# mLSTM cell and leaky-ReLU feed-forward: x of three steps of the second chunk transposed by VectorE and fetched through DRAM

## The chip, the core and the metric

The kernel runs on one core of a Trainium2 chip. The metric is the device time of one execution in microseconds. A core has five engines with instruction streams of their own: TensorE (PE: matrix products and transposes, with weight loads as PEld), VectorE (DVE), ScalarE (ACT), GpSimd (POOL) and SyncE (SP), which here does nothing but issue transfers between DRAM and the on-chip memory. ScalarE issues some transfers too. All transfers are carried out by sixteen DMA engines.

## The reference

An mLSTM cell runs over 4 batches, 8 heads, 768 positions and a head width of 40, and its output goes through two matrix products with a leaky ReLU between them:

```
m_new  = max(f + m, i)                      # gates, per head and position
C      = exp(f + m - m_new) * C + exp(i - m_new) * outer(v, k)
n      = exp(f + m - m_new) * n + exp(i - m_new) * k
y      = sigmoid(o) * (C q) / max(|n.q|, 1)
x      = y as (4 * 768 tokens, 320)
h      = x @ w_in                           # 320 -> 2048
out    = max(0.01 h, h) @ w_out             # 2048 -> 320
```

## The kernel before

The 768 positions are worked in six chunks of 128. A chunk has four steps, one per batch, so steps 0 to 3 are the first chunk, 4 to 7 the second, and so on to 23. A step yields x, 128 tokens by 320 columns. The feed-forward of a chunk takes its four steps together: `xT`, x transposed, with 512 tokens in the free dimension (step b of the chunk in columns 128 b to 128 b + 127), is multiplied by pieces of `w_in` (products `ph`), goes through the leaky ReLU into `acts`, and is multiplied by `w_out` (products `po`).

`xT` has five slots of 128 partitions by 512 tokens. Slot k holds rows 64 k to 64 k + 127 of the transposed x; the tile of x is 384 columns wide, with its first 64 columns repeated at the end, so that the last slot wraps round.

Cell and feed-forward are interleaved by hand: while the feed-forward of chunk c - 1 runs, the cell of chunk c is slipped in between. The loop at the end (L1471 to L1559) goes over the feed-forward's units i, runs unit i, then runs those units of the cell whose place is at most i. The list `cell_units` (L1270) says which units the cell of a chunk has, and `place` (L1461) where those of the second chunk stand. TensorE, VectorE, ScalarE and GpSimd execute in the order in which this code emits their instructions. SyncE's order is made by a scheduler, and stands fixed in the built program; there each of its transfers also waits for the one eight places before it.

For the second chunk (steps 4 to 7) the units of a step are `u_parts` (L707: scores and states on TensorE, their products on VectorE), `u_plain` (L776: the output `hN` on TensorE, its division by the denominator on VectorE and GpSimd, which gives the tile x, named `x` for steps 4 and 5 and `hn` for 6 and 7), and `u_x` (L851). `u_x` turns the 128x384 tile with five TensorE transposes (L860) into PSUM, from where ScalarE copies it into the step's columns of `xT` (L861, L862). All four `u_x` of the chunk come at the end, at places 22, 24, 26 and 28, when the feed-forward of the first chunk does its `po` products (L894).

Chunks three to six do it otherwise: their `u_mix` (L802) gives x already turned, writes it to the DRAM tile `x_dr`, and `gather_x` (L837) reads it from there into `xT`, both on SyncE's queue.

The next stage is `fast_firsts` (L1017) for the second chunk. Its first products (`p2`, then `p1`; matmuls at L1033) read the first 256 columns of `xT`, which are steps 4 and 5. Before it, `sums_of_x` (L1010) has GpSimd make sums of all four steps' columns (L1015); the third kind of product (`p6`) is the first to read those. `w_in` and `w_out` arrive as 64-bit numbers in the tile `raw` and are narrowed by ScalarE and VectorE (L302 to L311) in small pieces between the units. The loads for the third chunk (tiles `rb`, `ea`, `kn`, `S`, `w`) are issued on SyncE's queue while the second chunk's steps finish.

Of the kernel before, what the change touches and what calls it, by code (L numbers as in the profile page):

```python
# [8 lines left out]
F32 = mybir.dt.float32  # L9
# [9 lines left out]
def kernel(  # L19
# [26 lines left out]
    nc = tc.nc  # L46
    B, H, S, D = q.shape
    P = 128
# [5 lines left out]
    DP = 64  # L54
    D1 = D + 1
    QW = 32
    DB = D // 2
    XW = Dm + DP
    V1 = DB + 1
    TB = P // QW  # L60
# [5 lines left out]
    GT = B * P  # L66
    KF = Dm // P
    KR = Dm - KF * P
    KC = Dm // DP
# [10 lines left out]
    wk = ctx.enter_context(tc.tile_pool(name="wk", bufs=2))  # L80
    psf = ctx.enter_context(tc.tile_pool(name="psf", bufs=4, space=PSUM))
    psc = ctx.enter_context(tc.tile_pool(name="psc", bufs=4, space=PSUM))
    dr = ctx.enter_context(tc.tile_pool(name="dr", bufs=1, space=bass.MemoryType.DRAM))
# [17 lines left out]
    sync, by_act = queues = Ordered(nc.sync), Ordered(nc.scalar)  # L101
# [113 lines left out]
    raw_l = raw_t[:].bitcast(F32)  # L215
# [97 lines left out]

    a_dr = dr.tile([NB, 2, 2, BH, SL], F32, name="a_dr")
    x_dr = dr.tile([NS, Dm, P], F32, name="x_dr")
    gT, gL, dCs = {}, {}, {}
    m0s = {}
    bus = {}
# [68 lines left out]
    st = {}  # L387
# [449 lines left out]
    def gather_x(s):  # L837
# [6 lines left out]
        for r in range(2):  # L844
            at = 0
            while at < KC:
                k0, n = run_of(r, at)
                sync.dma_start(xT[DP * r : DP * (r + 1), at : at + n, ts(b, P)], src[:, k0 : k0 + n, :])
                at += n

    def u_x(s, last=None):  # L851

        c, b = divmod(s, B)
        if b == 0:
            st["xT", c] = wk.tile([P, KC, GT], F32, name="xT", bufs=1)
        x, xT, tok = st[s]["x"], st["xT", c], ts(b, P)
        low = psc.tile([P, 2, P], F32, name="xt", tag="c")
        high = psc.tile([P, KC - 2, P], F32, name="xe", tag="c")
        for t, n, at in ((low, 0, 0), (low, 1, DP), (high, 0, 2 * DP), (high, 1, 3 * DP), (high, 2, 4 * DP)):
            nc.tensor.transpose(t[:, n, :], x[:, at : at + P], ident[:])  # L860
        nc.scalar.copy(xT[:, :2, tok], low[:])  # L861
        (last or nc.scalar.copy)(xT[:, 2:, tok], high[:])  # L862
        if c > 0:
            del st[s]
# [404 lines left out]

    def cell_units(c):  # L1270
        if c == 1:
            units = [(fn, c * B + n) for n in range(B) for fn in (u_parts, u_plain)]
            units.insert(2 * B - 2, (u_gates, c + 1))
            return units + [(u_x, s) for s in range(B, 2 * B)]
        units = [(fn, c * B + n + m) for n in range(0, B, 2) for fn in (u_parts, u_mix) for m in range(2)]
        if c + 1 < NB:
            units.insert(2 * B - 2, (u_gates, c + 1))
        return units
# [57 lines left out]
    def first_chunk():  # L1336
# [49 lines left out]
        state(1)  # L1386
        run(w, 2)
        u_x(0)
        gate(1)
        run(w, 4)  # L1390
        u_x(1)
        state_copy(0)
        state_copy(1)
# [39 lines left out]
    with tc.manual_schedule(engines={E.PE, E.DVE, E.Activation, E.Pool}):  # L1433
# [24 lines left out]

        ffs = ffs[2:]
        fetch = {6: [3, 4], 10: [5, 6], 16: [7]}  # L1460
        place = (6, 7, 9, 11, 14, 16, 17, 19, 21, 22, 24, 26, 28)  # L1461
        late = {}
        masks = {0: (2, 3), 14: (4, 5)}
        first_pairs = (1, 1, 3, 3, 13, 13, 17, 17, 17)
# [6 lines left out]
        for c in range(1, NB + 1):  # L1471
            if c > 1:
                ffs = ff_units(c - 1)
            cells = cell_units(c) if c < NB else []
            n_ff, n_c = len(ffs), len(cells)
            done = fed = 0
# [19 lines left out]
            for i in range(n_ff):  # L1496
# [50 lines left out]
                while fed < done:  # L1547
                    fn, s = cells[fed]
# [42 lines left out]
```

## Time and profile before

| | us |
|---|---|
| median of 3 runs | 472.44 |
| lowest and highest | 471.0, 474.79 |
| the profiled execution | 471.96 |
| its span | 470.2 |

| engine | busy us | share of the span |
|---|---|---|
| TensorE, products | 459.6 | 98% |
| TensorE, weight loads | 412.5 | 88% |
| VectorE | 365.4 | 78% |
| ScalarE | 206.6 | 44% |
| GpSimd | 170.1 | 36% |

The profile is of one execution. Its times start at 0 with the span; the execution's own time has 1.8 us more than the span. Views that are quoted: the page's busy times and its forty slices (a digit is the busy share in tenths); the chain of waits in order of time (start, length, engine, tile and line, count); timelines (start, length, engine, line, operation, tiles written and read, count, and in brackets the idle time before and what ended it); and the DMA queues in a stretch of time (queue, packets, megabytes, share of sixteen engines). The granted TensorE clock is full throughout.

### The profile page before, as it was taken

The numbers are of one execution on the slowest core, as the hardware profiler recorded it, in microseconds if no ns is written. First come the engines' busy times: TensorE is split into PE (matmuls) and PEld (weight loads), VectorE is DVE, ScalarE is ACT, GpSimd is POOL, SyncE is SP. The second block draws the span as 40 slices with busy tenths as digits, with TensorE's granted clock in tenths as the row PEclk, the third lists the DMA queues.
The fourth block names the chain that finished last, engine by engine and source line by source line (L and its number), as shares of the span: only waits on it lengthen the run. The fifth ranks groups of instructions, "written<-read, shape, count | busy, mean of one in ns | idle before, by whom it ended". The sixth has DMA issues, their size and how long they took to land.

```text
span 470.2 us, 14195 instructions
## 1 busy us (share of the span) xinstructions
PE 459.6 (98%) x5700; PEld 412.5 (88%) x5700; DVE 365.4 (78%) x676; ACT 206.6 (44%) x507; POOL 170.1 (36%) x219
## 2 busy tenths in 40 slices
PE   8988989999999999999999999999999999999997
PEld 5777878767788999988899988899988899988997
DVE  6778578998579999768689778689757687495886
ACT  4657878755337511356411367411356411153410
POOL 6230487264335154933214933214833004400000
PEclk9999999999999999999999999999999999999999
DMA  9999977878742594865654956654776213100001
GB/s 128 169 179 179 214 181 230 207 158 164 147 141 55 151 181 107 186 141 134 166 133 84 197 127 140 179 110 100 176 142 125 75 30 85 57 1 1 1 1 56
DMA packets 160849, 59.21 MB, mean 126 GB/s; under 512 B 123792, under 2 KB 152208, under 8 KB 160784
## 3 DMA queue, kind: packets, MB, share of 16 engines
q1 hardware_dynamic: 120800, 51.15, 49.3%
q10 hardware_dynamic: 39984, 7.17, 9.3%
q8 instruction: 45, 0.74, 0.7%
q14 instruction: 20, 0.16, 0.1%
HBM read 51.58 MB, written 6.70 MB: 124 GB/s over the span
## 4 chain that ended last, share of the span: by engine, by line
PE 88%; DMA 5%; SPq 3%; POOL 1%; issue 1%; ACT 0%; DVE 0%; POOLq 0%; DVEq 0%
PE ph L1033 33%; PE po L931 26%; PE po L894 8%; PE pl L1236 6%; PE pT L813 3%; SPq L95 3%; PE ph L872 3%; PE sd L725 3%; DMA kn<-in_k_dram 3%; DMA acts<-in_moe_w_in_dram 1%; DMA w<-a_dr 1%; PE sd L731 1%; PE tk L638 1%; PE hN L785 1%; PE tkq L652 0%
## 5 line engine op out<-in xcount | busy, mean ns | idle before, releaser
L1033 PE MATMUL ph<-xT,w_in 64*128 64x256 f32 x720 | 82.7, 378 | 0.0
L1033 PEld LDWEIGHTS ph<-xT,w_in 64*128 64x128 f32 x720 | 69.2, 187 | 8.6 <-issue 0.6
L931 PE MATMUL po<-w_out,acts 128*128 128x160 f32 x512 | 71.3, 300 | 0.0
L931 PEld LDWEIGHTS po<-w_out,acts 128*128 128x128 f32 x512 | 69.9, 190 | 0.3
L1062 DVE TENSOR_TENSOR acts<-acts,ph 128x512 f32<-128x512 f32 x60 | 38.4, 683 | 22.8 <-PE ph L1033 22.7
L1066 ACT COPY acts<-ph 128x512 f32<-128x512 f32 x60 | 32.2, 588 | 49.7 <-PE ph L1033 49.7
L931 PE MATMUL po<-raw,acts 128*128 128x160 f32 x384 | 53.2, 300 | 0.0
L537 POOL TENSOR_SCALAR_AFFINE_SELECT w<-w 64x512 f32<-64x512 f32 x40 | 34.4, 861 | 51.3 <-DMA w<-a_dr 40.5
L931 PEld LDWEIGHTS po<-raw,acts 128*128 128x128 f32 x384 | 52.3, 190 | 0.3
L1058 ACT ACTIVATE acts<-acts 128x1024 f32<-128x1024 f32 x30 | 31.6, 1055 | 40.3 <-DVE acts L1062 30.8
L701 POOL TENSOR_TENSOR S<-S,f 40x336 f32<-40x336 f32 x36 | 30.6, 849 | 48.4 <-PE pT L813 32.7
L547 ACT ACTIVATE w<-w,gT 128x64 f32<-128x64 f32 x160 | 41.6, 337 | 13.1 <-DMA a_dr<-a 4.2
L742 DVE TENSOR_TENSOR qn<-w,sd 64x384 f32<-64x384 f32 (+1 forms) x80 | 33.4, 418 | 14.7 <-ACT acts L1066 7.8
L872 PE MATMUL ph<-xT,w_in 64*128 64x256 f32 x320 | 37.8, 383 | 0.0
L894 PE MATMUL po<-w_out,acts 128*128 128x320 f32 x128 | 36.7, 437 | 0.0
L1033 PE MATMUL ph<-acts,w 64*128 64x256 f32 x320 | 36.3, 379 | 0.0
L827 POOL TENSOR_TENSOR xb<-xb,den 128x320 f32<-128x320 f32 x16 | 11.6, 728 | 67.0 <-DVE xb L824 64.7
L872 PEld LDWEIGHTS ph<-xT,w_in 64*128 64x128 f32 x320 | 31.5, 187 | 3.8 <-ACT acts L880 0.4
L1033 PEld LDWEIGHTS ph<-acts,w 64*128 64x128 f32 x320 | 30.6, 187 | 3.6
L894 PEld LDWEIGHTS po<-w_out,acts 128*128 128x128 f32 x128 | 23.5, 190 | 9.2 <-ACT acts L880 0.3
L612 DVE TENSOR_TENSOR qn<-kqT,ea 64x512 f32<-64x512 f32 x32 | 30.0, 938 | 0.8
L1033 PE MATMUL ph<-xT,raw 64*128 64x256 f32 x240 | 26.8, 376 | 0.0
(267 smaller groups left out, 807.2 us busy)
## 6 DMA issues: line engine op xcount, KB each, us to landing
rb<-in_k_dram SPq DMA_DIRECT2D x64, 80.0 KB
rb<-in_q_dram SPq DMA_DIRECT2D x64, 80.0 KB
rb<-in_o_gate_dram SPq DMA_DIRECT2D x64, 80.0 KB
ea<-a_dr SPq DMA_DIRECT2D x32, 128.0 KB
raw<-in_moe_w_out_dram SPq DMA_DIRECT2D x6, 640.0 KB
w<-a_dr ACTq DMA_DIRECT2D x24, 128.0 KB
x_dr<-x SPq DMA_DIRECT2D x64, 40.0 KB
xT<-x_dr SPq DMA_DIRECT2D x16, 160.0 KB
```

Of the source, the lines that this page charges most:

```text
L537: nc.gpsimd.affine_select(part, part, compare_op=ALU.is_ge, fill=-1e30, base=0, pattern=[[0, H], [1, SL]], channel_multiplier=-1,)
L547: yield nc.scalar.activation(w[:, h, :], w[:, h, :], AF.Exp, bias=gT[c][:, 0, bh : bh + 1], scale=1.0)
L612: nc.vector.tensor_tensor(mixed(s)[rows, 1 - r], d["kqT"][rows, 1].rearrange("p (h t) -> p h t", t=SL), d["ea"][rows], op=ALU.mult,)
L701: nc.gpsimd.tensor_tensor(new, old, g, op=ALU.mult)
L742: nc.vector.tensor_tensor(mixed(s)[toks, u, hs], w[toks, hs], bank[1 - u][to[u][hs.start], hs], op=ALU.mult,)
L872: nc.tensor.matmul(ph[r][:, cols], lhsT=w_row(r, slot, j), rhs=xT[DP * r : DP * (r + 1), slot, cols], start=(slot == 0), stop=(slot == KC ...
L894: nc.tensor.matmul(po[n][:], lhsT=acts[:, f, ts(n, P)], rhs=w_out[:, f, :], start=(f == 0), stop=(f == NF - 1),)
L931: nc.tensor.matmul(bank[:], lhsT=left[:, f, :], rhs=right[:, f, :], start=f == 0, stop=f == KH - 1)
L1033: nc.tensor.matmul(bank[r][:, e, :], lhsT=left(r)[rows, e], rhs=right(r)[rows], start=first and e == 0 and m == 0, stop=e == 1 and m == le ...
L1058: nc.scalar.activation(to, z, AF.Prelu, alpha=0.01)
L1062: nc.vector.tensor_tensor(to[:, 2 * r : 2 * r + 2], to[:, 2 * r : 2 * r + 2], bank[r], op=ALU.add)
L1066: nc.scalar.copy(to[:, 2 * r : 2 * r + 2], bank[r])
```

## The change

For steps 4, 5 and 6 `u_x` is replaced by three units. `u_turn` has VectorE transpose the 128x384 tile of x in 32x32 blocks, each in its place, into a part of `raw` that the weights have left. `u_send` writes the blocks to a new DRAM tile `x1_dr`, one transfer for each of the four groups of 32 partitions; the blocks come to stand in DRAM in the order of the whole transpose, in pieces of 32 numbers (128 B). Steps 4 and 5 are sent together, step 6 alone. `u_gather` reads each step back into its columns of `xT` with one transfer over 128 partitions, five rows of 512 B in each, rows that belong to two slots being read twice. Step 7 keeps `u_x`. The places in the list are new: the transposes at 15 (twice) and 18, the sends at 16 and 19, the gathers at 19 and 20, the other units of the cell where they were, and the last `u_x` at 27 in place of 28.

```
+    x1_dr = dr.tile([B - 1, XW, P], F32, name="x1_dr")
...
+    def in_lines(s, n=1):
+        return raw_l[:, (s - B) * XW : (s - B + n) * XW]
+
+    def u_turn(s):
+        nc.vector.transpose(in_lines(s), st[s]["x"])
+        del st[s]
+
+    def u_send(s, n):
+        to = x1_dr[s - B : s - B + n].rearrange("b (j d) (i t) -> i d (b j) t", d=QW, t=QW)
+        for i in range(TB):
+            sync.dma_start(to[i], in_lines(s, n)[ts(i, QW)].rearrange("p (n t) -> p n t", t=QW))
+
+    def u_gather(s, n):
+        if s == B:
+            st["xT", 1] = wk.tile([P, KC, GT], F32, name="xT", bufs=1)
+        for n in range(s - B, s - B + n):
+            rows = bass.AP(x1_dr.tensor, x1_dr[n].offset, [[P, P], [DP * P, KC], [1, P]])
+            sync.dma_start(st["xT", 1][:, :, ts(n, P)], rows)
...
     def u_x(s, last=None):
         c, b = divmod(s, B)
-        if b == 0:
+        if s == 0:
...
         if c == 1:
-            units = [(fn, c * B + n) for n in range(B) for fn in (u_parts, u_plain)]
-            units.insert(2 * B - 2, (u_gates, c + 1))
-            return units + [(u_x, s) for s in range(B, 2 * B)]
+            (p0, x0), (p1, x1), (p2, x2), (p3, x3) = (((u_parts, s), (u_plain, s)) for s in range(B, 2 * B))
+            t0, t1, t2 = ((u_turn, s) for s in range(B, 2 * B - 1))
+            w01, w2 = ((lambda s, n=n: u_send(s, n), s) for s, n in ((B, 2), (B + 2, 1)))
+            g01, g2 = ((lambda s, n=n: u_gather(s, n), s) for s, n in ((B, 2), (B + 2, 1)))
+            t3 = u_x, 2 * B - 1
+            return [p0, x0, p1, x1, p2, t0, t1, w01, x2, (u_gates, c + 1), t2, p3, w2, g01, g2, x3, t3]
...
-        place = (6, 7, 9, 11, 14, 16, 17, 19, 21, 22, 24, 26, 28)
+        place = (6, 7, 9, 11, 14, 15, 15, 16, 16, 17, 18, 19, 19, 19, 20, 21, 27)
```

## The prediction

> **What bounds the kernel now.** I read the page first (busy times and slices), then the chain of waits over 80 to 180 us, then the timelines of TensorE, SyncE and VectorE around the four steps that the change touches, and last the trace's own records of DMA packets and of semaphore updates, which tell when each transfer landed.
>
> ```profile
> PE 459.6 (98%) x5700; PEld 412.5 (88%) x5700; DVE 365.4 (78%) x676; ACT 206.6 (44%) x507; POOL 170.1 (36%) x219
> PE   8988989999999999999999999999999999999997
> ```
>
> TensorE is full from the seventh slice on; in its own instructions the last gap over 0.04 us ends at 69 us. So from there the end is set by how much TensorE must do, and a piece taken out of it is worth its whole length, as long as nothing it later needs becomes late. The chain shows the pieces:
>
> ```profile
> 108.67 0.22 PE xt L860 x2
> 108.89 0.33 PE xe L860 x3
> 109.22 4.31 PE po L894 x16
> 113.52 0.22 PE xt L860 x2
> 113.74 0.33 PE xe L860 x3
> ...
> 123.78 2.15 PE po L894 x8
> 125.94 1.06 PE ph L1033 x8
> ```
>
> Each `u_x` is five transposes in 0.22 + 0.33 = 0.55 us. The last line is the first product of the next stage, the first reader of the second chunk's `xT`; its instruction starts at 125.87.
>
> **What it removes.** Three of the four `u_x`: 3 x 0.55 = 1.65 us of TensorE, all on the path. Their six ScalarE copies (373 and 482 ns each, 2.6 us) go as well; ScalarE waits there for the transposes, so they are worth nothing. The fourth `u_x` stays, one place earlier; its x is ready at about 114 us and TensorE doesn't wait for it. Without anything else the first product would start at 125.87 - 1.65 = 124.22.
>
> **What it adds to VectorE.** Three 32x32-block transposes of 128x384. No row has that shape; 128x512 took 690 ns at L604, 717 at L820 and 1140 at L831, whose output is scattered most. The new ones read and write plain rows, so I take L604's 384/512 x 690 = 0.52 us each, with 0.86 (from L831) as the upper end; nothing excludes a little less than 0.52, since all three rows have scattered sides. In the changed program's order two stand behind the L311 that ended at 90.76, the third behind the one at 98.82. VectorE has no idle time there until 107.69, so all that follows shifts by up to 3 x 0.52 = 1.56:
>
> ```profile
> 101.64 1.72 DVE L742 TENSOR_TENSOR qn<-w,sd 64x448 f32<-64x448 f32 x4
> 103.39 0.50 DVE L705 TENSOR_TENSOR S<-S,sd 40x336 f32<-40x336 f32 x1
> ```
>
> The L705 ends at 103.89, and TensorE's `hN` of step 7, which needs it, starts at 105.19. With 1.56 it ends at 105.45: TensorE waits about 0.3 us (with 0.86 per transpose, 1.3). At 107.69 VectorE had waited 0.98 for a weight load, so only 0.6 us is carried on, and its idle stretch after 124.65 (7.78 us) swallows that.
>
> **What it adds to SyncE's queue.** Eight writes and three gathers. In the program's order the four writes of steps 4 and 5 stand behind the first of the two `ea` loads of the first line below, the four of step 6 behind the `w` loads of the second, then the gathers, and the `rb` loads of the third only after them:
>
> ```profile
> 104.84 1.12 SPq L95 DMA_DIRECT2D ea<-a_dr  x2
> ...
> 114.29 1.28 SPq L95 DMA_DIRECT2D w<-a_dr  x2
> 115.66 2.01 SPq L95 DMA_DIRECT2D rb<-in_k_dram  x4
> ```
>
> SyncE issues without a pause there, one transfer per 0.35 to 0.65 us, so a place in the queue is a time. The blocks are ready long before (VectorE at about 91.8 and 100.4), so the queue decides. First `ea` issued at 105.4; four writes at the pace of four 32-partition loads (2.0) to 107.4; then what before took from 105.36 to 115.56 (10.2) to 117.6; four writes to 119.6; two gathers at the median 0.61 of `xT<-x_dr`, so the second starts at 120.2. Such gathers landed 3.1 to 5.1 us after the start of their issue (semaphore records, 169 to 178 us, a crowded stretch), the loads at 114 to 121 us 2.2 to 3.2. Between 3.2 and 5.1 the middle gives 124.4.
>
> The new packets lengthen this. The writes are 12 x 32 x 4 = 1536 packets of 128 B per step, 4608 in all. For their price, 111.5 to 116.5 us (mostly 80 B and 160 B loads) and 144 to 150 us (512 B writes to `x_dr`), queue, packets, MB and share of sixteen DMA engines:
>
> ```profile
> q1 hardware_dynamic: 3446, 0.57, 69.8%
> ...
> q1 hardware_dynamic: 548, 0.25, 17.3%
> ```
>
> The first is 0.698 x 16 x 5 us / 3446 = 16.2 ns for 165 B on average, the second 0.173 x 16 x 6 / 548 = 30.3 ns. The packet records agree: median 12 ns at 80 B, 14 at 160 B, 18 for the 256 B writes of `a_dr`. I take 14 ns, by size the nearest row: 4608 x 14 / 16 = 4.0 us of all engines. The idle share between 105.4 and 120 is 13% and 29% in the table by stretches, 0.6 + 2.9 = 3.5 us. So the writes fit but for 0.5 us, and the gather of step 5 **lands at about 125.0** (124.4 + 0.5). Each further ns per packet adds 4608 / 16 = 0.29 us.
>
> The Trainium skill, "DMA: Bandwidth & Descriptors", Specifications, says that transfers under 512 B make the engine read, modify and write; it speaks against these 128 B writes. If that doubled a packet to 28 ns, the sum would end at a landing of 129.0. The 256 B writes at 18 ns don't bear it out.
>
> **The sum.** TensorE reaches the first product at 125.87 - 1.65 + 0.3 = 124.5 and waits for the listed semaphores of the gathers of steps 4 and 5 until about 125.1. The start moves from 125.87 to 125.1: **a gain of about 0.75 us** of the 1.65. The two waits share: a longer one at `hN` shortens the other. The gather of step 6 waits for its writes to land (issued to 119.6, landing at 122.4 or so) and lands near 126; it and the remaining `u_x` feed GpSimd's sums, which in the run before started at 125.31 and are first read by TensorE at 138.88. Ten us of cover.
>
> Behind the gathers the queue is about 7 us late (2.0 + 2.0 + 3 x 0.61, and the wait of about 1.5 for landings). The tightest is step 11's `w`, landed at 130.61 before, 138 after; GpSimd's masks (L537, at 130.56) stand in front of its L701 at 137.64, which VectorE reads at 142.44. Masks until 139, L701 until 140: covered. The loads for VectorE's transposes at 148 to 153 landed by 134.4, so they have over 10 us.
>
> The profiled execution took 471.96 (span 470.2 and 1.8 around it), which the sum makes 471.2. The median of the runs is 472.44, 0.5 above that execution; against it, **471.7 us**.
>
> **The rivals.**
> - *The gather comes too late, slower than before.* One mechanism: the first product waits for the gather of step 5, and what passes 125.8 is a loss. It decides at a packet price of 14 + 0.8 / 0.29 = 17 ns. At the 30.3 ns of the `x_dr` writes the landing is 125.0 + 16.3 x 0.29 = 129.7, a loss of 3.9 us: 476.3. For it: those are this kernel's writes of x to DRAM, and SyncE has at most eight transfers under way, as each waits in the program's list for the one eight before it, so a slow write also holds up the issue. Against it: the packets grow dearer with size, and the 256 B writes cost 18. By the Trainium skill's rule (28 ns) the loss would be 3.2 us, 475.6. Chance 0.35.
> - *All of the 1.65 us but the 0.3 is kept.* The gathers land after 3.2 us as the lightly crowded loads did, by 124.5: 471.1. It belongs to the forecast's side, of which it is the better end.
> - *A covered wait loses its cover:* the transposes at 0.86 us and SyncE's 7 us grown to over 10, so that the masks hold L701, then VectorE's state and, at 161 us, TensorE's scores. No TensorE reader comes earlier, so it costs 0 to 3 us, 472 to 475. Chance 0.07.
> - *The transposes stay or the work moves elsewhere:* the program's order shows 15 fewer transposes before the first product, so no chance is kept for it.
>
> **How the numbers follow.** The forecast with its better end, net -1.65 to 0, has 0.55; the late gather 0.35; lost cover 0.07; 0.03 is left for what I don't see. The range runs from 470.2 (the full 1.65 off the median, and 0.6 for a median of few runs that spread from 471.0 to 474.79) to 476.0, nearly the late gather at 30.3 ns. A measurement of this kernel can tell about 1%, 4.7 us. A gain over 1% isn't in the work removed: 0.03. A loss over 1% needs a landing after 130.6, a packet price of 33 ns (the median of single `x_dr` packets is 34), or several losses together: 0.11. Within 1%: 0.86.
>
> **What would show it.** 15 fewer L860 transposes in the chain and 16 `po` matmuls following one another without them; the three new block transposes near 0.52 us; `hN` of step 7 waiting 0.3 us for VectorE; the first product waiting under 1 us for a DMA into `xT`; SyncE's `rb` loads starting near 122.5 in place of 115.66. It is wrong if that product waits over 1.5 us, or if TensorE has gaps after 126 us.

## The result and the profile after

| | before | after |
|---|---|---|
| median, us | 472.69 (6 runs) | 493.40 (6 runs) |
| lowest and highest | 471.0, 474.79 | 490.29, 499.72 |
| the profiled execution | 471.96 | 499.72 |
| its span | 470.2 | 497.9 |

The changed kernel is slower by a factor of 1.0425, with a 95% interval of 1.0375 to 1.0476: 20.7 us of the median, where the forecast was a gain of 0.75 and the range ended at 476.0. The profiled execution is the longest of the six, so its own loss is larger, 27.7 us of span; e1_both below shows the same later waits in an execution near its median. Ratios and intervals, here and below, leave out single executions far above the others of their kernel: 499.72 here, one of the kernel before at 530.78 and one of e8_softpin at 2672 us.

The page of the kernel after: busy times, two of the rows of forty slices (TensorE's busy tenths and the clock that it was granted), and the shares of the chain that ended last. Line numbers move with every edit (L1015 of the kernel before is L1039 here), and the profile leaves numbers out of tile names, so that `x1_dr` stands in it as `x_dr`.

```profile
PE 467.0 (94%) x5685; PEld 417.8 (84%) x5685; DVE 364.7 (73%) x679; ACT 203.9 (41%) x501; POOL 162.7 (33%) x219
PE   8998999999699999899999599999849999999997
...
PEclk9999999999799999999999979999959999999999
...
PE 59%; DMA 17%; SPq 14%; DVE 4%; POOL 3%; issue 2%; ACT 1%; ACTq 0%; DVEq 0%; POOLq 0%
```

TensorE's row had been full from the seventh slice on. Now it has dips in the slices 11, 17, 23 and 29 to 30, one at each start of a stage but the last, and the clock's row has dips in 11, 24 and 30. Although 15 products have gone, TensorE is busy for 7.4 us longer, since part of its work ran at half clock. The waits of TensorE (for whom; us in total, times, the longest) put names to the dips. The kernel before has neither of the two:

```profile
PE ph L1057 <- POOL acts L1039: 16.0, 3, 7.8
PE ph L1057 <- DMA xT<-x_dr: 4.3, 1, 4.3
```

The second line is the first product of the second chunk, which waits for the gather of step 5 at 124.81. The first line is the greater part, and it lies in stages that the change didn't touch. At the starts of the chunks 3, 4 and 5 the products `p6` (L1057) wait for GpSimd's sums (L1039): 1.63 us at 208.07, 6.65 at 280.27, 7.75 at 359.61. The sums wait for the gathers of those chunks, which GpSimd's own timeline shows at the third chunk, first before, without a wait, then after (start, length, line, and in brackets the idle time before and what ended it):

```profile
193.00 1.27 POOL L1015 TENSOR_TENSOR acts<-xT 128x512 f32<-128x512 f32 x1
...
205.69 1.27 POOL L1039 TENSOR_TENSOR acts<-xT 128x512 f32<-128x512 f32 x1 [6.99 <-DMA xT<-x_dr]
```

The last term is the clock. The table by stretches of the kernel after: us, then busy time and instructions of each engine (TensorE, its weight loads, VectorE, ScalarE, GpSimd), the granted clock, DMA share and GB/s.

```profile
124.80:129.20 4.40, 0.05 (x3) 0.08 (x2) 3.37 (x10) 0.43 (x1) 0.00 (x0) 0.82 0.92 243
129.20:134.40 5.20, 5.20 (x24) 4.48 (x26) 0.00 (x0) 0.00 (x0) 3.79 (x3) 0.50 0.96 197
134.40:139.00 4.60, 4.60 (x156) 4.07 (x152) 0.66 (x2) 2.15 (x4) 2.53 (x3) 1.00 0.75 133
```

Behind the gap TensorE gets 24 products done in 5.2 us at a clock of 0.50. In the kernel before, the first 5.2 us of this stage (125.9 to 131.1) have 49. The clock records give three such intervals: 127.61 to 134.44, 284.63 to 291.45 and 363.13 to 373.37. What lies behind the end of each gap is 5.28 + 4.53 + 6.01 = 15.8 us, half of it lost: 7.9 us. The balance of this execution is 20.4 us of gaps (4.35 + 1.63 + 6.65 + 7.75) + 7.9 of clock - 1.65 of transposes + 0.6 (TensorE was free at 124.81, not at 124.22) = 27.2, of 27.7.

So the question is why gathers of later chunks, whose code is the same, are issued late. In the kernel before the six gathers of steps 8 and 9 were issued from 169.61 on, in the kernel after from 185.76 on, though the stage began only 3.3 us later. SyncE's issue of those gathers in the kernel before, and its waits there between 110 and 380 us:

```profile
169.61 6.48 SPq L95 DMA_DIRECT2D xT<-x_dr  x6
...
SPq L95 <- DVE x L831: 21.7, 8, 8.5
SPq L95 <- DMA S<-in_v_dram: 18.8, 16, 3.7
```

Then the waits of the kernel after:

```profile
SPq L95 <- DMA S<-in_v_dram: 62.3, 24, 9.3
SPq L95 <- DMA w<-a_dr: 12.2, 10, 3.6
```

SyncE was ahead of its data before: its longest wait was for x. Now it spends 62.3 us waiting for loads of v into `S` to land, with which a gather of x has nothing to do. Those loads are issued by ScalarE. The timeline of the kernel after between 183 and 192 us, SyncE's first (start, length, engine, line, operation, tiles, count):

```profile
185.20 0.45 SPq L95 DMA_DIRECT2D ea<-a_dr  x1
185.76 7.30 SPq L95 DMA_DIRECT2D xT<-x_dr  x6
```

And ScalarE's there:

```profile
182.90 0.29 ACT L1002 COPY hn<-po 128x160 f32<-128x160 f32 x1 [6.15 <-PE po L955]
182.91 0.60 ACTq L1358 DMA_DIRECT2D S<-in_v_dram  x1
...
187.25 0.29 ACT L987 COPY y<-po 128x160 f32<-128x160 f32 x1 [1.88 <-PE po L955]
187.26 0.60 ACTq L1358 DMA_DIRECT2D S<-in_v_dram  x1
...
189.42 0.29 ACT L987 COPY y<-po 128x160 f32<-128x160 f32 x1 [1.88 <-PE po L955]
189.43 0.60 ACTq L1358 DMA_DIRECT2D S<-in_v_dram  x1
```

ScalarE executes in order. Each load of v stands behind a copy that waits for TensorE's next `po`, one every 2.17 us. The load issued at 182.91 landed at 185.18, and SyncE's second `ea` went out at 185.20 after a wait of 5.1 us. The load issued at 187.26 landed at 189.88, and a gather went out at 189.89. This is a chain through TensorE, ScalarE and SyncE that no data calls for.

The built programs show where it comes from. The transfers of SyncE and those of ScalarE share eight lanes (semaphores that count landings). A scheduler puts both into one common order at build time, and each transfer waits until the one eight places before it has landed, whichever engine issued that. (The description of the kernel before, and the prediction, have this for SyncE's list alone.) With eleven transfers more on SyncE, that order came out another way. The six first gathers of the third chunk stood at the places 202 to 210, with none of v's loads of that block ahead of the first of them. After the change they stand at 220 to 228: eleven places for the new transfers, and seven more for loads of v that are now ahead of them. In the chunks 4 and 5, where the two long gaps lie, all sixteen of v's loads behind the previous chunk's gathers stand ahead of the chunk's first gather, where the kernel before had 11 and 12 of them (e8_softpin, below, has 8 and 8). Those gathers begin 21.7 and 31.3 us later than before, in stages that begin 7.6 and 16.6 us later. Why the scheduler came to this order, and not another, was not looked into.

### The profile page after: what moved, and what is told of

It reads as the page before. It is cut to its first block, busy times and chain, and to the rows that moved or that the text cites. A ratio compares the mean times of both kernels' runs of the same rounds, so it can differ in the third digit from the quotient of the medians.

```text
span 497.9 us, 14173 instructions
## 1 busy us (share of the span) xinstructions
PE 467.0 (94%) x5685; PEld 417.8 (84%) x5685; DVE 364.7 (73%) x679; ACT 203.9 (41%) x501; POOL 162.7 (33%) x219
## 4 chain that ended last, share of the span: by engine, by line
PE 59%; DMA 17%; SPq 14%; DVE 4%; POOL 3%; issue 2%; ACT 1%; ACTq 0%; DVEq 0%; POOLq 0%
PE ph L1057 31%; PE po L955 15%; SPq L95 14%; PE pl L1260 6%; DMA S<-in_v_dram 4%; PE pT L814 3%; DMA xT<-x_dr 3%; DMA w<-a_dr 2%; DMA raw<-in_moe_w_out_dram 2%; DMA a_dr<-a 2%; POOL acts L1039 2%; PE sd L726 1%; DMA rb<-in_q_dram 1%; DMA x_dr<-x 1%; DMA kn<-in_k_dram 1%
## 5 line engine op out<-in xcount | busy, mean ns | idle before, releaser
L1057 PE MATMUL ph<-xT,w_in 64*128 64x256 f32 x720 | 85.6, 386 | 4.3 <-DMA xT<-x_dr 4.3
L1057 PEld LDWEIGHTS ph<-xT,w_in 64*128 64x128 f32 x720 | 72.2, 192 | 12.9 <-issue 5.0
L1057 PE MATMUL ph<-acts,w 64*128 64x256 f32 x320 | 41.8, 419 | 16.0 <-POOL acts L1039 16.0
L1057 PEld LDWEIGHTS ph<-acts,w 64*128 64x128 f32 x320 | 34.1, 210 | 22.2 <-POOL acts L1039 17.2
L538 POOL TENSOR_SCALAR_AFFINE_SELECT w<-w 64x512 f32<-64x512 f32 x40 | 31.3, 781 | 50.4 <-DMA w<-a_dr 39.6
L896 PE MATMUL ph<-xT,w_in 64*128 64x256 f32 x320 | 37.9, 383 | 1.0 <-DVE S L690 0.5
L896 PEld LDWEIGHTS ph<-xT,w_in 64*128 64x128 f32 x320 | 31.5, 187 | 5.0 <-PE ph L896 0.9
L821 DVE STREAM_TRANSPOSE hb<-pT 128x512 f32<-128x512 f32 x16 | 11.5, 717 | 32.6 <-PE pT L814 32.5
L1057 PE MATMUL ph<-xT,raw 64*128 64x256 f32 x240 | 27.2, 376 | 0.0
```

The costliest lines, as they stand in the source:

```text
L538: nc.gpsimd.affine_select(part, part, compare_op=ALU.is_ge, fill=-1e30, base=0, pattern=[[0, H], [1, SL]], channel_multiplier=-1,)
L896: nc.tensor.matmul(ph[r][:, cols], lhsT=w_row(r, slot, j), rhs=xT[DP * r : DP * (r + 1), slot, cols], start=(slot == 0), stop=(slot == KC ...
L1057: nc.tensor.matmul(bank[r][:, e, :], lhsT=left(r)[rows, e], rhs=right(r)[rows], start=first and e == 0 and m == 0, stop=e == 1 and m == le ...
```

## The experiments

Three theories were stated. **Re-merge:** the other common order makes the later gathers wait for loads of ScalarE's. **Lateness:** the late start of the second chunk is handed on and grows. **Load:** eleven transfers more, and x on its way through DRAM, are late whatever the order. In the table, "ahead" is the number of v's loads in the common order ahead of the third chunk's first gather, counted from the loads for that chunk on; "SP on v" is SyncE's waiting for v's loads between 110 and 380 us; "first" the gap before the second chunk's first product, "later" the gaps before `p6` in the chunks 3 to 5, "half clock" the sum of the intervals, all of the profiled execution. Medians and ratios to the kernel before are of the timed runs.

| kernel | ahead | SP on v | first | later | half clock | median | ratio, 95% interval |
|---|---|---|---|---|---|---|---|
| before | 0 | 18.8 | 0 | 0 | 0 | 472.2 to 472.7 | 1 |
| after | 7 | 62.3 | 4.35 | 16.0 | 23.9 | 493.4 | 1.0425 (1.0375 to 1.0476) |
| e1_both | 7 | 67.7 | 0 | 15.8 | 17.1 | 493.95 | 1.0476 (1.0439 to 1.0513) |
| e3_early | 8 | 69.8 | 0.85 | 18.4 | 23.9 | 499.4 | 1.0580 (1.0556 to 1.0605) |
| e6_fill | 6 | 51.2 | 0 | 8.0 | 13.7 | 488.6 | 1.0344 (1.0318 to 1.0370) |
| e2_pin | 0 | 18.9 | 2.20 | 0 | 3.4 | 479.8 | 1.0156 (1.0124 to 1.0187) |
| e4_pin_early | 0 | 14.4 | 2.11 | 0 | 0 | 478.1 | 1.0116 (1.0091 to 1.0141) |
| e7_pin_before | 0 | 10.2 | 0 | 0 | 0 | 475.2 | 1.0048 (1.0029 to 1.0068) |
| e5_delay | 0 | 18.0 | 0 | 0 | 0 | 483.0 | 1.0227 (1.0202 to 1.0252) |
| e9_softpin_early | 0 | 32.1 | 0.71 | 0 | 0 | 472.8 | 1.0008 (0.9987 to 1.0028) |
| e8_softpin | 0 | 31.6 | 0.35 | 0 | 0 | 473.2 | 1.0004 (0.9978 to 1.0030) |
| e12_softpin_before | 0 | 17.8 | 0 | 0 | 0 | 471.6 | 0.9991 (0.9969 to 1.0012) |

(The profile columns of e8_softpin are those of e8b_softpin_again, the same kernel.)

### The path through DRAM walked for nothing: e1_both

```
-        del st[s]                                        # u_turn keeps x
...
+        scrap = raw_l[:, 4 * Dm :][:, : KC * 3 * P].rearrange("p (k t) -> p k t", k=KC)
-            sync.dma_start(st["xT", 1][:, :, ts(n, P)], rows)
+            sync.dma_start(scrap[:, :, ts(n, P)], rows)
...
-            t3 = u_x, 2 * B - 1
+            xs = [(u_x, s) for s in range(B, 2 * B)]
```

The four `u_x` stand at 22, 24, 26 and 28 again.

> The kernel after with all fifteen of before's TensorE transposes of steps 4 to 6 put back, so that xT 1 is filled by u_x as before; the way through DRAM is still walked (the same transposes on VectorE, stores and gathers), but its gathers go to a scrap part of a buffer and nothing reads them. The first product of the second chunk then waits for no gather. Re-merge theory (the eleven DMAs more change the order in which the transfers of SP and ACT share their lanes, so that the xT gathers of the chunks 3 to 5 stand behind v's loads, which ScalarE issues late): the waits of p6 for POOL acts L1039 ahead of chunks 3 to 5 stay, 14 to 18 us of TensorE gaps in all and a lowered clock behind the two long ones; no gap at the first product; no gain of 1.65 us; 486 to 493 us. Lateness theory (the first wait alone is handed on and grows): no wait at the first product, so none later; 472 to 475 us.

TensorE's waits of e1_both, and then SyncE's between 110 and 380 us:

```profile
PE ph L1055 <- POOL acts L1037: 15.8, 3, 8.1
```

```profile
SPq L95 <- DMA S<-in_v_dram: 67.7, 28, 6.4
```

No wait at the first product, which starts at 125.17 (125.87 before), and still 493.95 us, a little above the upper end of what the re-merge theory gave. Of the span's 21.0 us over the kernel before, 20.7 are the three later gaps, 15.8, and the clock behind two of them, (4.3 + 5.5) / 2 = 4.9. The first wait, the only thing that the prediction's sum had looked at, isn't needed for the loss. The lateness theory falls here.

### Lateness without the change: e5_delay

```
+                if c == 2 and i == 0:
+                    late_bank = psc.tile([P, Dm], F32, name="late", tag="c")
+                    for _ in range(21):
+                        nc.tensor.matmul(late_bank[:], lhsT=ident[:], rhs=w_out[:, 0, :], start=True, stop=True)
                 ffs[i]()
```

> The kernel before, with 21 products of 128x512 into a bank that nobody reads, ahead of the second chunk's first product: 21 x some 0.25 us, about 5.7 us of TensorE's time more, which makes everything behind the first product late by what the wait of the kernel after made it late, without a change of SP's work. The merged order of the transfers keeps the gathers of the third chunk ahead of nearly all of v's loads. Re-merge theory: 5.7 us and no new gap: 477 to 480 us, the stage starts all later by one constant. Lateness theory: the gaps before the chunks 3 to 5 come up here too: 486 to 496 us.

Each product went out in two pieces of 320 columns, 42 pieces between 126.9 and 138.3 us, so the delay was some 11.4 us, twice what was meant, and the time is up by 10.4. The number missed its range for that reason; the test is the stronger for it. Later stages follow at the old distances (138.26, 210.86, 281.20, 351.39, 419.48: 72.6, 70.3, 70.2 and 68.1 us, before 72.8, 70.3, 70.3 and 68.1), and there is no new gap. Lateness alone costs itself and nothing more.

### The order restored by force: e2_pin and e4_pin_early

Every load of ScalarE's for the later chunks (w, kn, v) is ordered behind the gathers that were emitted before it.

```
+        order["xT"] = sync.ins.name                      # at the end of gather_x
...
+    def behind_gathers(made):
+        if "xT" in order:
+            tc.add_manual_dep(made.ins, order["xT"], ISSUED, reason="issue order")
+        return made
...
-                yield nc.scalar.dma_start(w[...], ...)   # and kn, and S
+                yield behind_gathers(nc.scalar.dma_start(w[...], ...))
```

> The kernel after, with one thing added: each load that ScalarE issues for the chunks from the third on (w, kn, v) is ordered by the scheduler behind the xT gathers that SP has been given before it in the program, by an order without a wait. That puts the six first gathers of the third chunk at the places 212 to 217 of the common order of transfers with none of v's loads ahead of them, as in the kernel before (202 to 210). Re-merge theory: the gaps before the chunks 3 to 5 vanish (POOL's sums L1039 start within 8 us of before's 193.0, 263.4, 335.5); the gap of 3 to 5 us at the first product and the lowered clock behind it stay; 475 to 481 us. Lateness theory: the gaps stay, 489 to 495 us. Theory of the load (eleven transfers more on SP's queue and a later turn of x are late whatever the order): the gaps stay at half or more, 485 to 494 us.

The later gaps are away, SyncE's waiting for v is back at 18.9 us, and the time falls from 493.4 to 479.8, with the eleven transfers all in place. This is the re-merge theory's result, and the load theory's at least for the greater part falls. Still 7 us remain, more than the first wait of 2.20 explains.

e4_pin_early has the gathers of steps 4 and 5 one place sooner as well:

```
-            return [p0, x0, p1, x1, p2, t0, t1, w01, x2, (u_gates, c + 1), t2, p3, w2, g01, g2, x3, t3]
+            return [p0, x0, p1, x1, p2, t0, t1, w01, x2, (u_gates, c + 1), g01, t2, p3, w2, g2, x3, t3]
...
-        place = (6, 7, 9, 11, 14, 15, 15, 16, 16, 17, 18, 19, 19, 19, 20, 21, 27)
+        place = (6, 7, 9, 11, 14, 15, 15, 16, 16, 17, 18, 18, 19, 19, 20, 21, 27)
```

> The edit of e2_pin, and the gathers of steps 4 and 5 one place earlier: ahead of the third step's transpose and send, at the place 18. Those gathers are then issued some 3 us earlier (two stores, and whatever they wait for, come after them), so the first product, which waited 4.35 us, waits 0 to 1.5 us. Re-merge theory: the whole of the loss is away and the change shows its 1.65 us: 470.5 to 475 us. Lateness theory: also 470.5 to 475 us, since the first wait is away; it is e2_pin and e1_both that tell the two apart. Theory of the load: 482 to 491 us.

478.1 us, above what the re-merge theory gave. The first wait didn't shrink (2.11 us), since SyncE was late in this execution before the change's first transfer, and the second stage took 78.2 us, 5.4 more than before. ScalarE's waits of e4_pin_early between 125 and 206 us say why:

```profile
ACT raw L975 <- DMA ea<-a_dr: 8.4, 1, 8.4
ACT hn L1003 <- DMA x_dr<-x: 8.3, 1, 8.3
```

The coupling works in both directions. Held behind the gathers, ScalarE's own transfers now wait for SyncE's `ea` and `x_dr` transfers, and its copies stand behind them.

### The order edit by itself: e7_pin_before

The edit of e2_pin on the kernel before.

> The kernel before with the order edit of e2_pin alone (w, kn and v of the later chunks behind SP's gathers). e2_pin and e4_pin_early were 5 to 7 us over the kernel before, with 5.4 us of it in the second chunk's stage (78.2 us from its first product to the third chunk's against 72.8), where ScalarE's copies stood behind its own transfers that waited for SP's. If that is the price of the order edit: 475 to 478.5 us, with the longer second stage. If it is the price of the eleven transfers: 472 to 474 us.

475.2 us, 0.48% above the kernel before (0.29% to 0.68%, 1.4 to 3.2 us), at the lower edge of the first case: the forced order has a price of its own. Its second stage took 75.1 us where before had 72.8, and one of ScalarE's copies waits 8.7 us there for a transfer into `x_dr`. It is part of what e2_pin and e4_pin_early kept; the rest of their 5 to 7 us isn't explained by this run.

### Sooner gathers without the order: e3_early

The second edit of e4_pin_early alone.

> The kernel after with the gathers of steps 4 and 5 at the place 18, ahead of the third step's transpose and send, and nothing else. In the common order of transfers the third chunk's first gathers stand at 221 to 229, with all eight of v's loads ahead of them. The first wait shrinks from 4.35 us to 1 to 3 us (it was 2.1 us in e4_pin_early). Re-merge theory: the three later gaps stay, 14 to 18 us in all, two of them with the clock lowered behind them: 487 to 493 us. Lateness theory: with the first wait halved the later gaps halve too or go: 474 to 484 us.

TensorE's waits of e3_early:

```profile
PE ph L1057 <- POOL acts L1039: 18.4, 3, 7.7
...
PE ph L1057 <- DMA xT<-x_dr: 0.9, 1, 0.9
```

The first wait is down to 0.85 us, and the kernel is slower than the kernel after, 499.4 us (above the range given). One more of v's loads stands ahead of the gathers, and the later gaps are longer. That a smaller first wait comes with larger later gaps is the opposite of lateness.

### The first wait filled with work: e6_fill

e5_delay's edit with 8 products, on the kernel after.

> The kernel after with 8 products of 128x640 (16 of 128x320, some 0.27 us each in e5_delay, so 4.2 us) ahead of the second chunk's first product, into a bank that nobody reads: TensorE works through the time in which it waited 4.35 us. If a gap of TensorE is what the granted clock falls upon, no interval of half clock lies at 127 to 135 us any more, and PE's busy time there is shorter by some 2.5 us; the two intervals behind the later gaps stay: 488 to 493 us. If the clock falls for another reason (the load of DMAs, the place in the program), the interval is still there.

The clock records of e6_fill have no interval of half clock at 127 to 135 us any more, and two behind the later gaps, as was expected if gaps lower the clock. The time, 488.6, lies in the range, but it isn't a clean measure of the clock's price: the common order changed again (six of v's loads ahead in place of seven), and the later gaps fell to 8.0 us. In the three kernels with seven or eight ahead they are 15.8 to 18.4, in those with none there are none.

### A weaker order: e9_softpin_early and e8_softpin

Only v's loads are ordered, behind the first transfer of a block of gathers; w and kn stay free.

```
+                if at == 0 and r == 0 and b == 0:        # in gather_x
+                    order["xT"] = sync.ins.name
...
-                    yield nc.scalar.dma_start(S_v[...], ...)
+                    yield behind_gathers(nc.scalar.dma_start(S_v[...], ...))
```

> The kernel after with the gathers of steps 4 and 5 at the place 18 and a weaker order: only v's loads are ordered, and only behind the first transfer of the latest block of gathers; w and kn stay where they were. The third chunk's gathers then stand at 213 to 224 with two to three of v's loads between them, as before (202 to 210), and kn ahead of them. Re-merge theory, with the price of e4_pin_early laid to the held back kn and w: the second stage is back at 73 to 74 us, the first wait is 1 to 2.5 us, no later gap over 2 us: 471.5 to 475 us. If the eleven transfers themselves make the second stage longer: 476 to 480 us.

472.8 us, even with the kernel before (1.0008, 0.9987 to 1.0028), and the second stage at 74.4 us. e9_softpin_early also has the sooner gathers; e8_softpin hasn't, so it is the change itself with the order mended:

> The kernel after with the weak order of e9_softpin_early (v's loads of the later chunks behind the first transfer of the latest block of gathers), and its gathers of steps 4 and 5 where the change put them. What it is over the kernel before is the price of the first wait alone. Re-merge theory: a wait of 2 to 4.5 us at the first product, behind it 0 to 3 us for a lowered clock, no other gap over 2 us, less up to 1.65 us for the transposes that are gone: 473.5 to 478 us.

473.2 us, ratio 1.0004 (0.9978 to 1.0030), just under the range given. This is the decisive run: the same three transposes on VectorE, the same eleven transfers, their gathers at the same places in the list, and 20 us less than the kernel after. All that can be measured of the loss was the order: what the kernel keeps of it lies between -1.0 and +1.4 us. A second profile of this kernel:

> The kernel of e8_softpin once more, for its profile alone: e8_softpin's own profile is of an execution in which every engine ran several times slower than in its other eleven, and says nothing of them. Its time was even with the kernel before (ratio 1.0004), so the first wait together with the clock behind it should be no more than the 1.65 us that the transposes gave plus some 1.5 us of noise: a gap of 0 to 3 us before the second chunk's first product, no interval of half clock or one of 3.4 us, and no later gap over 2 us. If the gap is as long as in the kernel after (4.35 us, 6.8 us of half clock), the kernel must have gained in a later stage what it lost there.

The page of e8b_softpin_again (471.11 us; TensorE's row and its clock), then its waits of SyncE between 110 and 380 us:

```profile
PE 459.7 (98%) x5685; PEld 412.8 (88%) x5685; DVE 367.3 (78%) x679; ACT 204.3 (44%) x501; POOL 163.8 (35%) x219
...
PE   9888999999999999999999999999999999999997
...
PEclk9999999999999999999999999999999999999999
```

```profile
SPq L95 <- DMA S<-in_v_dram: 31.6, 23, 3.4
```

TensorE is full again and the clock whole; the first product waits 0.35 us, where 2 to 4.5 were expected of e8_softpin. SyncE still waits 31.6 us for v's loads, since six of them stand between the first and the last of a block of six gathers, but no wait is longer than 3.4 us, and GpSimd's sums start at 193.5, 262.7 and 333.7 (before: 193.0, 263.4, 335.5).

### The weak order on the kernel before: e12_softpin_before

> The kernel before with the weak order alone, x of all four steps turned by TensorE. The third chunk's first gathers stand where they stood, at 202 to 210. If the weak order is worth nothing in itself: 471.5 to 473 us, and e9_softpin_early's tie with the kernel before is the change's own balance. If it gives something that the change takes back: 469 to 471 us.

471.6 us, 0.9991 (0.9969 to 1.0012): the weak order is worth nothing by itself. So e8_softpin's tie is the change's own balance: what it gains of its 1.65 us is below what these runs can tell, and none of the versions is faster than the kernel before.

### The path begun sooner: e10_order_sooner

This is e9_softpin_early with its units in another order and at other places; the places are shown.

```
-        place = (6, 7, 9, 11, 14, 15, 15, 16, 16, 17, 18, 19, 19, 19, 20, 21, 27)
+        place = (6, 7, 9, 11, 13, 13, 13, 14, 16, 16, 16, 17, 18, 19, 20, 21, 27)
```

> e9_softpin_early with the way through DRAM begun sooner: the two first transposes and their send at the place 13 in place of 15 and 16, the gathers of steps 4 and 5 at 16, at 104 and 105 of the common order of transfers where they were at 120 or later. They should land 8 us sooner, so that the first product waits for none (it waited 0.7 us). If that wait was what ate the gain: 470.5 to 472 us, faster than the kernel before by up to 1.65 us. If the gain is lost elsewhere (VectorE's transposes put back its work for TensorE, 0.9 us at the place of the second stage where TensorE waited for acts; SP stands behind the gathers while the stores land): 472 to 475 us.

490.5 us (1.0380, 1.0348 to 1.0412), and nothing of what was expected. At the place 13 the part of `raw` that takes the blocks is still in use by weights of `w_out` that are being narrowed. Blocks and weights get in each other's way, the products of `w_out` are computed from partly other numbers, and the time is that of another calculation. In time, ScalarE's write into `raw` had to wait for the stores that read it, and TensorE for VectorE behind it. The waits of e10_order_sooner between 80 and 112 us:

```profile
ACT raw L303 <- DMA x_dr<-raw: 18.3, 1, 18.3
...
PE tg L377 <- DVE hn L794: 16.9, 1, 16.9
```

The gathers did land sooner, at 110.5 us, and the later stages have no gaps. Whether a sooner path with a buffer of its own would show the 1.65 us wasn't tried.

## Why the prediction was wrong, point by point

**What it removes: right.** Fifteen transposes are gone, and in e8b_softpin_again TensorE is free for the first product at 124.41, where the sum had 124.5.

**VectorE: right.** The timeline of the kernel after has the new transposes at 0.52 us each (two together) and 0.56:

```profile
91.17 1.04 DVE L858 STREAM_TRANSPOSE raw<-x 128x384 f32<-128x384 f32 x2
...
100.85 0.56 DVE L858 STREAM_TRANSPOSE raw<-hn 128x384 f32<-128x384 f32 x1
```

The L706 that `hN` of step 7 needs ended at 104.95, not 105.45, and TensorE didn't wait there; the 0.3 us of the sum were none.

**The packets: right, and the first rival's price was wrong.** The 128 B writes took 12.9 ns on average (median 13), against 14 taken and the 17 from which that rival decides. The prediction had also priced a packet doubled to 28 ns, an assumption of its own that it hung on a rule of the Trainium skill; no packet doubled. The rule itself (the Trainium skill, "DMA: Bandwidth & Descriptors", Specifications) has 512 B as the least transfer for the full rate, and below it a read, a modification and a write. The trace agrees with the first part: the 512 B packets of the new gathers took 29 ns on average (median 27), so that a byte of the 128 B writes cost 1.8 times as much. Whether anything was read and modified, no run here shows. One reading was off: the 13% idle of the DMA engines between 105.4 and 110 is the mean from 100 on, and in steps of five microseconds the table gives 105 to 110 a share of 1.13, which leaves no idle time there.

**SyncE's timetable: its steps right to 1.7 us, its origin not.** From the first `ea` to the gather of step 5 the sum had 15.4 us (104.84 to 120.2); in the five executions with the gathers where the change put them it is 16.4 to 17.1, the landing 3.8 to 4.0 us behind the issue in place of 4.8 (with the 0.5 for the packets). The four first writes took 4.3 us in the kernel after and 3.3 in e8b_softpin_again, not 2.0: the third stands behind a weight load eight places before it, which landed at 110.46 in the kernel after. These errors nearly cancel: in e8b_softpin_again the `rb` loads behind the gathers went out at 122.09, near the forecast 122.5. But the first `ea` itself, at the same place of the same stream, was issued between 104.36 and 108.28 us in the twelve profiles in which the hundred transfers up to it are the same, and the sum had taken 104.84 from one of them, with 0.8 us between its landing (125.0) and a loss (125.8). In the kernel after the `rb` loads went out at 126.28. Four of the twelve profiles are without the change (104.67 to 106.32), eight with it (104.36 to 108.28); whether the transposes on VectorE add to the lateness is not shown. The chains of the kernel after and of e8b_softpin_again, first one, then the other, show the two ends of that:

```profile
125.04 3.98 DMA xT<-x_dr
129.02 0.14 issue
129.15 1.19 PE ph L1057 x3
```

```profile
120.76 3.86 DMA xT<-x_dr
124.62 0.14 issue
124.75 5.42 PE ph L1059 x47
```

In the second the first product waits 0.35 us, as forecast (landing at 124.62, forecast 125.0); in the first it waits 4.35. The failed step is "so a place in the queue is a time", read off a single execution. It was the smaller error.

**The step that failed: "Behind the gathers the queue is about 7 us late", with every reader covered.** It moved SyncE's later transfers by a constant and looked for the first reader who would notice. But a place in the queue also decides whose landing a transfer waits for. The prediction knew the eight places and counted them in SyncE's list alone; the lanes are shared with ScalarE. The later gathers came 16 us late (169.6 to 185.8) in a stage that began 3.3 us late, 16.0 us of TensorE's gaps followed, and the clock behind them. None of this was in the sum or in a rival, and the range ended at 476.0. That this order was the cause, e8_softpin shows: with the order mended, 473.2 in place of 493.4. The common order could have been read from the built program before any run.

**The clock: not in the sum.** A gap of TensorE was priced at its length. Behind gaps of 4.35, 6.65 and 7.75 us another 2.6, 2.3 and 3.0 us were lost.

**The rivals.** The late gather had the right mechanism for the first gap, with another cause (SyncE's origin, not the packets), and its 3.9 us are a fifth of the 20.7. The lost cover had VectorE's state at 142 us in mind; the cover that was lost was that of the gathers, from the third chunk on. "If TensorE has gaps after 126 us" was the sign that the text named for being wrong, and it is what the page shows.

## What to carry to other kernels

Before transfers are added to a queue, compare the built programs' common order of transfers over all the engines that share its lanes: in this kernel that order alone, with the same work, was worth 20 us, and a weak order on one engine's loads took the loss away. Time taken from the bounding engine is only as safe as the waits that replace it, and a slack of 0.8 us on a queue whose dates differ by 4 us from one profile to the next is none. Price a gap of TensorE of more than 2 us at its length and some 2 to 3 us of lowered clock behind it, as in this kernel.

## What the runs showed of the hardware that was not expected

**The granted clock falls within short gaps.** Thirteen profiles together, each gap of TensorE of more than 2 us behind the first 70 us of a run, with the interval of half clock that went with it:

| gap, us | half clock, us |
|---|---|
| 2.11, 2.50 | none |
| 2.20, 3.23 | 3.41 |
| 2.77, 4.35, 4.97, 5.24, 6.65 | 6.83 |
| 7.41, 7.71, 7.75, 8.06 | 10.24 |
| 16.86 | 20.48 |

The intervals are whole multiples of 3.41 us, begin 2 to 4.4 us after the gap's beginning and end 3.4 to 6.2 us after its end. The Trainium skill ("TensorE: Matmul & The Clock Gate", What's actually happening) has a free-running window of 3413 ns, by which TensorE's activity is judged, and half rate after an idle window of that length. The trace agrees with the window: the intervals of one execution begin on one grid (in the kernel after 157.02 and 78.50 us apart, 46 and 23 times 3.413). It differs on the idle time: 2.20 us lowered the clock, 2.11 and 2.50 didn't. What decides is how much of a gap falls into one window of the grid. Behind the first 70 us of the thirteen profiles, the clock fell at the end of every window with 2.06 us or more of TensorE's idle time, and of none with 1.86 or less. It came back at the end of the first window with 0.03 us or less, and stayed at half through those with 0.65 or more. The gap of 2.50 us lay across two windows, 0.78 and 1.72 us in each; the one of 2.20 lay in a single window.

**SyncE's dates differ from one profile to the next more than those of TensorE.** The same 99 transfers put the next one at 104.4 to 108.3 us, with single issues of 2.1 us where the same place takes 0.5 in other profiles, while TensorE, in the ten of these executions without delay products, came to the end of the first stage between 123.8 and 125.9, with and without the 1.65 us of transposes.
